# Decode attention over two KV caches: score products of the "D" heads shared between Pool and DVE, and the query weights laid into the V buffer

## The chip, the cores and the metric

The kernel runs on one core of a Trainium2 chip. Its time is the device time of one execution in microseconds (us). A profile is one execution; its span is 1.7 to 2.0 us shorter than the measured time of the same execution. The engines are named as the profile names them: PE does the matrix products, ACT and DVE copy, multiply and reduce, Pool multiplies, and SP issues the loads. SBUF is the memory that the loads fill; PSUM is the one that PE writes its products to.

## The reference, cut to what matters

Two independent problems, A and B, are the same single-token attention. Each has 32 heads, 8192 keys and a head size of 128, all bf16:

```python
q = (x @ wq).reshape(B, Sq, H, Dh).transpose(0, 2, 1, 3)          # x: 1 x 512, wq: 512 x 4096
scores = einsum("bhqd,bhkd->bhqk", q, k_cache) * Dh ** -0.5       # k_cache: 32 x 8192 x 128
o = einsum("bhqk,bhkd->bhqd", softmax(scores), v_cache)
out = o.transpose(0, 2, 1, 3).reshape(B, Sq, H * Dh) @ wo         # wo: 4096 x 512
```

There are 64 heads in all, and each needs a K block and a V block of 2 MB. Nothing is reused, so with the weights wq and wo 285 MB have to be read for a few vector products. The question of every such kernel is whether the loads ever stop.

## The kernel before

The heads go through in periods. In period g the K block of head g is loaded and its scores are computed, and the V block of head g - 12 is loaded and multiplied with its probabilities ("PV", on PE). Eight heads make a round, and each round has one softmax. K blocks go round in four buffers and V blocks in three. All loads are issued by SP in a fixed order, and a load first waits until the user of its buffer's former content is done:

```python
        def load_k(g):
            slot = g % NK                                  # NK = 4
            if g >= NK:
                ctr, val = k_free[g - NK]
                W('SP', ctr, val)
            ...
        def load_v(g):
            slot = g % NV                                  # NV = 3
            if g >= NV:
                W('SP', c_pv, pv_val[g - NV])
            ...
```

Scores are computed on one of two paths. A "P" head is transposed by PE, copied out of PSUM by ACT and multiplied by PE. A "D" head is multiplied with the broadcast query by Pool, in eight chunks of 128 x 1024, and reduced by DVE:

```python
            OP('POOL', lambda e, ...: e.tensor_tensor(
                ybuf[:, ys], kn[:, slot, i * CH:(i + 1) * CH, :],
                qbc[:, buf, qi:qi + 1, :].broadcast_to([P, CH, Dh]), ALU.mult
            ).then_inc(c_mul.sem, 1), "mul(%d,%d)" % (g, i))
            W('DVE', c_mul, mv)
            ...
            OP('DVE', lambda e, ...: e.tensor_reduce(
                s_sb[:, rb, j, i * CH:(i + 1) * CH], ybuf[:, ys], AX.X, ALU.add
            ).then_inc(c_red.sem, 1), "red(%d,%d)" % (g, i))
```

Which head takes which path is a string of 64 letters. Before, it is PPDPPDPPDPPD and then D and P by turns: 34 P heads and 30 D heads, head 62 D and head 63 P.

Each engine runs its own list of instructions in order. PE's list holds, one after the other, the transposes and score products of head g, the PV of head g - 12, and, now and then, the small products of a softmax. One of these, the transpose of the round's maxima, waits for DVE:

```python
        def plan_sm_tr(r, m1v):
            W('PE', c_m1, m1v)          # DVE's maxima of all eight heads of the round
            ...
            OP('PE', lambda e: e.transpose(misc[:, 0:P], m1pad[:], ident_f[:]).then_inc(c_x1.sem, 1), "smtr(%d)" % r)
```

Of the kernel before, what the change touches and what calls it, by code (L numbers as in the profile page):

```python
# [27 lines left out]
def _default_path(NG, G, LAG):  # L28
    pre = "PPDPPDPPDPPD"
    out = []  # L30
    for g in range(NG):
        if g < len(pre):
            out.append(pre[g])
        else:
            out.append("D" if (g % 2 == 0) else "P")
    return "".join(out)[:NG]


def bass_concat_heads__mha_block_cached__gqa_block_cached__decode_kernel(
# [15 lines left out]
    NV: int = 3,  # L55
# [4 lines left out]
    SMD: tuple = (2, 2, 2, 2, 2, 3, 2, 1),  # L60
):
# [5 lines left out]
    NA = 2  # L67
# [48 lines left out]
    with ExitStack() as st:  # L116
# [3 lines left out]
        vn = ec(nc.sbuf_tensor("vn", [P, NV, NT, Dh], BF16))  # L120
        ktsb = ec(nc.sbuf_tensor("ktsb", [P, NU, UT * P], BF16))
        ybuf = ec(nc.sbuf_tensor("ybuf", [P, NY, CH, Dh], BF16))
        wq_sb = ec(nc.sbuf_tensor("wq_sb", [P, NC_, H * Dh], BF16))
# [22 lines left out]
        y_acc = ec(nc.sbuf_tensor("y_acc", [1, NA, NOUT], F32))  # L146
        out_sb = ec(nc.sbuf_tensor("out_sb", [1, NA, NOUT], BF16))
        NKB = 3
        ktps = ec(nc.psum_tensor("ktps", [P, NKB, UT * P], BF16))
        sps = ec(nc.psum_tensor("sps", [P, 2, 512], F32))  # L150
# [19 lines left out]
        c_red = C("c_red")  # L170
        c_m1 = C("c_m1")
# [20 lines left out]

        def W(eng, ctr, val):
            if val is None or val <= 0:
                return
            prog[eng].append(lambda e, c=ctr, v=val: e.wait_ge(c.sem, v))
            DEBUG_PLAN.setdefault(eng, []).append("wait %s>=%d" % (ctr.name, val))
# [87 lines left out]
        def load_k(g):  # L285
            slot = g % NK
            if g >= NK:
                ctr, val = k_free[g - NK]
                W('SP', ctr, val)
# [4 lines left out]
        def load_v(g):  # L294
            slot = g % NV
            if g >= NV:
                W('SP', c_pv, pv_val[g - NV])
            a, h = divmod(g, H)
# [68 lines left out]
        def plan_T(g, u):  # L367
# [12 lines left out]
            if u == UPH - 1:  # L380
                k_free[g] = (c_t, tv)
# [47 lines left out]
        chunk_count = [0]  # L429

        def plan_D_chunk(g, i):
            n = chunk_count[0]
            chunk_count[0] = n + 1
            slot = g % NK
            ys = n % NY
# [3 lines left out]
            if i == 0:  # L439
                W('POOL', s_kn[slot], k_land[g])  # L440
                W('POOL', c_qbe, qbc_ready[g])
            if n >= NY:
                W('POOL', c_red, n - NY + 1)
            mv = c_mul.bump()
            assert mv == n + 1
            if i == NMC - 1:
                k_free[g] = (c_mul, mv)
            OP('POOL', lambda e, slot=slot, ys=ys, i=i, buf=buf, qi=qi: e.tensor_tensor(  # L448
                ybuf[:, ys], kn[:, slot, i * CH:(i + 1) * CH, :],
                qbc[:, buf, qi:qi + 1, :].broadcast_to([P, CH, Dh]), ALU.mult  # L450
            ).then_inc(c_mul.sem, 1), "mul(%d,%d)" % (g, i))
            W('DVE', c_mul, mv)
            if i == 0 and r >= 2:
                W('DVE', c_p, p_val[(r - 2) * G + G - 1])
            rv = c_red.bump()
            assert rv == n + 1
            if i == NMC - 1:
                red_last_val[g] = rv
            OP('DVE', lambda e, ys=ys, rb=rb, j=j, i=i: e.tensor_reduce(  # L459
                s_sb[:, rb, j, i * CH:(i + 1) * CH], ybuf[:, ys], AX.X, ALU.add  # L460
            ).then_inc(c_red.sem, 1), "red(%d,%d)" % (g, i))
# [189 lines left out]
        def plan_og_final(oi):  # L651
# [27 lines left out]
            if lastgrp:  # L679
                if first:  # L680
                    OP('DVE', lambda e: e.tensor_copy(out_sb[:, a, :], misc[0:1, 0:NOUT]).then_inc(c_y.sem, 1), "y(%d)" % oi)
                else:
                    OP('DVE', lambda e: e.tensor_tensor(out_sb[:, a, :], y_acc[:, a, :], misc[0:1, 0:NOUT], ALU.add).then_inc(c_y.sem, 1), "y(%d)" % oi)
                out_pending.append((a, yv))
            else:
                if first:
                    OP('DVE', lambda e: e.tensor_copy(y_acc[:, a, :], misc[0:1, 0:NOUT]).then_inc(c_y.sem, 1), "y(%d)" % oi)
# [222 lines left out]
```

## Time and profile before

| what | value | where it is read |
|---|---|---|
| time | 701.4 us (median of 3), 702.0 us (median of 15 in all) | runs |
| span of the profiled run | 703.0 us | page |
| bytes read, mean rate | 285.2 MB, 407 GB/s | page |
| DMA queue busy | 97.4% of the span | page |
| Pool, PE, ACT, DVE busy | 72, 72, 50, 45% | page |

These are the page's lines of busy time (us, share of the span, instructions), of the DMA queue (packets, MB, share of 16 engines), and of the two groups of the D path (busy us, mean ns of one, idle before it and what ended the idle time).

```profile
...
PE 505.2 (72%) x5915; PEld 325.7 (46%) x6000; DVE 314.1 (45%) x397; ACT 349.8 (50%) x583; POOL 504.1 (72%) x254
...
q1 hardware_dynamic: 28868, 285.23, 97.4%
...
L448 POOL TENSOR_TENSOR ybuf<-kn,qbc 128x1024 bf16<-128x1024 bf16 x240 | 499.8, 2119 | 129.6 <-DMA kn<-in_A_k_cache_dram 65.5
L459 DVE TENSOR_REDUCE s_sb<-ybuf 128x8 f32<-128x1024 bf16 x240 | 292.2, 1219 | 280.4 <-POOL ybuf L448 280.2
...
```

The DMA queue is nearly always busy and no engine is, so the loads bound the kernel. What can be won are the places where the loads stop. They are found by cutting the span into stretches of 5 us. This is the view of busy time by windows for the kernel before; the last three columns are the granted PE clock (as a share of the full clock), the DMA share and the GB/s.

```profile
...
core 0: us, PE busy (x) PEld busy (x) DVE busy (x) ACT busy (x) POOL busy (x), PEclk, DMA share, GB/s
...
55.00:60.00 5.00, 4.43 (x90) 3.46 (x88) 2.44 (x2) 5.00 (x7) 3.92 (x3) 1.00 0.61 202
...
600.00:605.00 5.00, 1.30 (x4) 0.48 (x5) 3.08 (x4) 0.00 (x0) 5.00 (x4) 0.55 1.00 423
...
635.00:640.00 5.00, 4.74 (x70) 3.04 (x68) 1.69 (x10) 3.50 (x4) 0.00 (x0) 1.00 0.60 206
...
665.00:670.00 5.00, 4.53 (x28) 1.99 (x28) 0.32 (x2) 0.90 (x2) 0.00 (x0) 1.00 0.88 311
...
```

The stretch from 600 us is what an undisturbed one looks like: a DMA share of 1.00 and 423 GB/s. From 55 to 60 us and from 635 to 640 us the loads were idle four tenths of the time, and from 665 to 670 us over one tenth. The next view lists what SP, which issues the loads, waited for (total us, times, longest).

```profile
...
SPq L238 <- PE acc L601: 468.8, 61, 12.9
SPq L238 <- PE ktps L387: 61.2, 14, 19.3
SPq L238 <- POOL ybuf L448: 41.6, 6, 14.6
...
```

SP waits nearly all the time, which is as it should be while loads are queued. It says who can make the loads stop: PE, which frees the V buffers (acc) and the K buffers of P heads (ktps), and Pool, which frees the K buffers of D heads. The same view cut to 34 to 62 us has one wait for Pool, of 10.6 us, and it belongs to the first D head: Pool needs 8 x 2.12 = 17 us for it, from 40.7 us on, and the next K load is issued at 57.4. The hole at 55 us is this wait.

To compare kernels at a given time I add up the bytes from stretches of 20 us (GB/s times 20 us). The kernel before has 38.9 MB at 100 us, 249.7 MB at 600 us and 273.4 MB at 660 us. One MB is 2.3 us at 427 GB/s.

### The profile page before, as it was taken

How to read it: one execution, taken by the hardware profiler on the slowest of the kernel's cores; microseconds unless marked ns; L12 is line 12 of the kernel's file. 1: busy time of each engine (PE TensorE's matmuls, PEld its weight loads, DVE VectorE, ACT ScalarE, POOL GpSimd, SP SyncE). 2: the span in 40 equal slices, each digit the busy share in tenths (PEclk: the TensorE clock that was granted, in tenths of full speed). 3: DMA queues.
4: the chain of work that ended last, by engine and by line, in shares of the span. 5: the costliest groups of instructions: out<-in, count | busy, mean ns of one | idle time of the engine just before them, and what ended most of it. 6: DMA issues, size and time to landing. Idle time of an engine off the chain costs nothing.

```text
span 703.0 us, 14000 instructions
## 1 busy us (share of the span) xinstructions
PE 505.2 (72%) x5915; PEld 325.7 (46%) x6000; DVE 314.1 (45%) x397; ACT 349.8 (50%) x583; POOL 504.1 (72%) x254
## 2 busy tenths in 40 slices
PE   1866567958687576767868675886777678769876
PEld 1765554725455343444535344553434445445332
DVE  0035446565454645444554534556454445542001
ACT  0837666727565272645625365552726457336010
POOL 2069799998788888876898858888787868980000
PEclk9967757968989898998989899898989989889999
DMA  8999999999999999999999999999999999998993
GB/s 338 420 413 356 412 407 425 398 428 413 430 427 410 427 430 423 429 413 426 425 424 415 420 425 426 427 412 428 425 429 414 400 428 424 428 412 345 382 418 149
DMA packets 28929, 286.11 MB, mean 407 GB/s; under 512 B 3266, under 2 KB 11460, under 8 KB 11460
## 3 DMA queue, kind: packets, MB, share of 16 engines
q1 hardware_dynamic: 28868, 285.23, 97.4%
q8 instruction: 47, 0.77, 0.4%
q14 instruction: 14, 0.11, 0.0%
HBM read 285.21 MB, written 0.00 MB: 406 GB/s over the span
## 4 chain that ended last, share of the span: by engine, by line
DMA 53%; POOL 18%; PE 15%; ACT 6%; issue 4%; DVE 1%; another core or an unknown queue 1%; SPq 1%; ACTq 0%; DVEq 0%
DMA kn<-in_B_k_cache_dram 25%; DMA kn<-in_A_k_cache_dram 22%; POOL ybuf L448 18%; PE acc L601 7%; DMA vn<-in_B_v_cache_dram 4%; PE ktps L387 4%; ACT ktsb L396 3%; PE misc L665 3%; ACT ptmp L546 2%; DMA wq_sb<-in_A_wq_dram 2%; PE sps L420 1%; SPq L238 1%; PE acc L312 1%; DVE s_sb L459 0%
## 5 line engine op out<-in xcount | busy, mean ns | idle before, releaser
L448 POOL TENSOR_TENSOR ybuf<-kn,qbc 128x1024 bf16<-128x1024 bf16 x240 | 499.8, 2119 | 129.6 <-DMA kn<-in_A_k_cache_dram 65.5
L459 DVE TENSOR_REDUCE s_sb<-ybuf 128x8 f32<-128x1024 bf16 x240 | 292.2, 1219 | 280.4 <-POOL ybuf L448 280.2
L396 ACT COPY ktsb<-ktps 128x1024 bf16<-128x1024 bf16 x272 | 264.3, 1023 | 70.3 <-PE ktps L387 63.5
L601 PE MATMUL acc<-vn,pt 128*128 128x512 bf16 x940 | 280.2, 414 | 20.3 <-DMA vn<-in_B_v_cache_dram 8.4
L387 PE MATMUL ktps<-ident,kn 128*128 128x128 bf16 x2176 | 181.7, 233 | 42.8 <-DMA kn<-in_B_k_cache_dram 25.6
L387 PEld LDWEIGHTS ktps<-ident,kn 128*128 128x128 bf16 x2176 | 153.2, 105 | 101.9 <-DMA kn<-in_B_k_cache_dram 33.1
L620 ACT CAST accsb<-acc 4x512 bf16<-4x512 f32 x64 | 36.6, 572 | 230.3 <-PE acc L601 224.5
L601 PEld LDWEIGHTS acc<-vn,pt 128*128 128x128 bf16 x1024 | 88.2, 105 | 86.8 <-issue 34.5
L420 PE MATMUL sps<-q_sb,ktsb 128*128 128x8 bf16 (+1 forms) x2176 | 95.9, 168 | 21.0 <-ACT ktsb L396 15.3
L420 PEld LDWEIGHTS sps<-q_sb,ktsb 128*128 128x128 bf16 x2176 | 83.9, 98 | 41.6 <-ACT ktsb L396 35.1
L665 PE MATMUL misc<-wo_sb,ot_pad 128*128 128x512 bf16 x64 | 26.8, 591 | 29.0 <-DVE ot_pad L648 29.0
L497 PE MATMUL misc<-ident_f,m1pad 128*128 128x128 f32 x8 | 3.6, 456 | 40.1 <-DVE m1pad L487 40.1
L648 DVE CAST ot_pad<-acc 128x1 bf16<-128x1 f32 x64 | 9.6, 150 | 50.4 <-PE acc L632 50.4
L665 PEld LDWEIGHTS misc<-wo_sb,ot_pad 128*128 128x128 bf16 x64 | 8.2, 136 | 45.0 <-DVE ot_pad L648 32.1
L577 ACT ACTIVATE pt<-ptmp,rinv 128x64 bf16<-128x64 f32 x64 | 16.1, 334 | 12.3 <-DVE rinv L564 12.3
L497 PEld LDWEIGHTS misc<-ident_f,m1pad 128*128 128x128 f32 x8 | 1.4, 176 | 44.1 <-DVE m1pad L487 44.1
L632 PE MATMUL acc<-ej,accsb 128*128 128x8 bf16 x256 | 16.2, 169 | 4.1 <-ACT accsb L620 1.8
L312 PE MATMUL acc<-xT,wq_sb 128*128 128x1 bf16 x256 | 7.0, 165 | 16.4 <-DMA wq_sb<-in_A_wq_dram 14.9
L324 DVE CAST q_sb<-acc 128x32 bf16<-128x32 f32 x2 | 0.4, 192 | 38.9 <-PE acc L312 38.9
L632 PEld LDWEIGHTS acc<-ej,accsb 128*128 128x128 bf16 x256 | 12.7, 100 | 10.2 <-ACT accsb L620 8.7
L344 ACT ACTIVATE diag<-ident,q 128x128 bf16<-128x128 bf16 x30 | 9.7, 403 | 12.6 <-DVE q L326 12.6
L312 PEld LDWEIGHTS acc<-xT,wq_sb 128*128 128x128 bf16 x256 | 6.9, 102 | 16.4 <-issue 16.4
(36 smaller groups left out, 86.3 us busy)
## 6 DMA issues: line engine op xcount, KB each, us to landing
kn<-in_A_k_cache_dram SPq DMA_DIRECT2D x32, 2048.0 KB, 18.0
vn<-in_A_v_cache_dram SPq DMA_DIRECT2D x32, 2048.0 KB, 15.6
kn<-in_B_k_cache_dram SPq DMA_DIRECT2D x32, 2048.0 KB, 19.3
vn<-in_B_v_cache_dram SPq DMA_DIRECT2D x32, 2048.0 KB, 13.6
wq_sb<-in_A_wq_dram SPq DMA_DIRECT2D x1, 4096.0 KB, 12.9
wq_sb<-in_B_wq_dram SPq DMA_DIRECT2D x1, 4096.0 KB, 17.2
wo_sb<-in_A_wo_dram SPq DMA_DIRECT2D x4, 1024.0 KB, 19.2
wo_sb<-in_B_wo_dram SPq DMA_DIRECT2D x4, 1024.0 KB, 18.8
```

The costliest lines, as they stand in the source:

```text
L312: last = e.matmul(acc[:, a, h:h + 1], wq_sb[:, c, h * Dh:(h + 1) * Dh], xT[:, a * NC_ + c:a * NC_ + c + 1], start=(c == 0), stop=(c == NC_ ...
L387: last = e.transpose(ktps[:, bank, i * P:(i + 1) * P], kn[:, slot, t, :], ident[:])
L396: OP('ACT', lambda e, bank=bank, ks_slot=ks_slot: e.copy(ktsb[:, ks_slot, :], ktps[:, bank, :]).then_inc(c_e.sem, 1), "evac(%d,%d)" % (g, u))
L420: last = e.matmul(sps[:, sb, col:col + nn], ktsb[:, ks_slot, i * P:(i + 1) * P], q_sb[:, g:g + 1].broadcast_to([P, nn]), start=True, stop= ...
L448: OP('POOL', lambda e, slot=slot, ys=ys, i=i, buf=buf, qi=qi: e.tensor_tensor(ybuf[:, ys], kn[:, slot, i * CH:(i + 1) * CH, :], qbc[:, buf ...
L459: OP('DVE', lambda e, ys=ys, rb=rb, j=j, i=i: e.tensor_reduce(s_sb[:, rb, j, i * CH:(i + 1) * CH], ybuf[:, ys], AX.X, ALU.add).then_inc(c_ ...
L546: OP('ACT', lambda e, r=r, j=j, g=g, rb=rb: e.activation(ptmp[:, rb, j, :], s_src(g), AF.Exp, bias=negb[:, r, j:j + 1], scale=scale, accum ...
L577: OP('ACT', lambda e, r=r, j=j, rb=rb: e.activation(pt[:, rb, j * NT:(j + 1) * NT], ptmp[:, rb, j, :], AF.Copy, scale=rinv[:, r, j:j + 1], ...
L601: last = e.matmul(acc[:, ob, :], pt[:, rb, j * NT + c * PVC:j * NT + c * PVC + P], vn[:, slot, c * PVC:(c + 1) * PVC, :].rearrange("p t d ...
L620: OP('ACT', lambda e, ob=ob: e.copy(accsb[0:PVC, ob, :], acc[0:PVC, ob, :]).then_inc(c_ac.sem, 1), "acccopy(%d)" % g)
L632: last = e.matmul(acc[:, ob, 0:NB], accsb[:, ob, jj * Dh:(jj + 1) * Dh], ej[:, jj:jj + 1].broadcast_to([P, NB]), start=(jj == 0), stop=(jj ...
L665: last = e.matmul(misc[:, 0:NOUT], ot_pad[:, g - r * G, :], wo_sb[:, r % 2, g - r * G, :], start=(i == 0), stop=(i == n - 1),)
```

## The change

Its intent: give Pool only six of a D head's eight chunks and let DVE multiply the other two, so that more heads (40 and not 30) can leave PE and ACT, and so that a D head frees its K buffer earlier. DVE reads the query from a copy in PSUM, which PE builds once per round. PSUM room for it comes from the transposes' buffer (two banks and not three). The query weights wq move into the space of the V buffers, which are idle while wq is needed; the room saved pays for a fourth V buffer.

```diff
-    pre = "PPDPPDPPDPPD"
+    pre = "PDPDPPDPDPDP"
...
-            out.append("D" if (g % 2 == 0) else "P")
+            out.append("P" if (g % 3 == 2) else "D")
...
-    NV: int = 3,
+    NV: int = 4,
...
+    DVC: int = 2,
...
+        wq_sb = vn[:, 0:WQS].rearrange("p s t d -> p (s t d)")[:, 0:NC_ * H * Dh].rearrange("p (c n) -> p c n", c=NC_)
...
-        wq_sb = ec(nc.sbuf_tensor("wq_sb", [P, NC_, H * Dh], BF16))
+        ybufe = ec(nc.sbuf_tensor("ybufe", [P, NYE, CH, Dh], BF16))
+        qrep = ec(nc.sbuf_tensor("qrep", [P, MAXD, P], BF16))
...
-        NKB = 3
+        NKB = 2
+        qps = ec(nc.psum_tensor("qps", [P, UT * P], BF16))
...
+            if g < WQS:
+                W('SP', c_q, q_done_val[NA - 1])
...
+                OP('DVE', lambda e, slot=slot, es=es, i=i, qs=qs: e.tensor_tensor(
+                    ybufe[:, es], kn[:, slot, i * CH:(i + 1) * CH, :],
+                    qps[:, None, qs * P:(qs + 1) * P].broadcast_to([P, CH, Dh]), ALU.mult
+                ).then_inc(c_dmul.sem, 1), "dmul(%d,%d)" % (g, i))
...
+            if r >= 1:                     # in the building of the PSUM copy for round r
+                prev = [h_ for rr in range(r) for h_ in round_D[rr]]
+                if prev:
+                    W('PE', c_dmul, dmul_val[(prev[-1], NMC - 1)])
```

The new path string makes head 62 a P head and head 63, the last one, a D head.

More of the change, by code (lines that the diff above doesn't have):

```diff
@@ L120, in bass_concat_heads__mha_block_cached__gqa_block_cached__decode_kernel @@
         vn = ec(nc.sbuf_tensor("vn", [P, NV, NT, Dh], BF16))
+        WQS = (NC_ * H * Dh + NT * Dh - 1) // (NT * Dh)
+        assert WQS <= NV
+        wq_sb = vn[:, 0:WQS].rearrange("p s t d -> p (s t d)")[:, 0:NC_ * H * Dh].rearrange("p (c n) -> p c n", c=NC_)
         ktsb = ec(nc.sbuf_tensor("ktsb", [P, NU, UT * P], BF16))
         ybuf = ec(nc.sbuf_tensor("ybuf", [P, NY, CH, Dh], BF16))
-        wq_sb = ec(nc.sbuf_tensor("wq_sb", [P, NC_, H * Dh], BF16))
+        NYE = 2
+        ybufe = ec(nc.sbuf_tensor("ybufe", [P, NYE, CH, Dh], BF16))
+        qrep = ec(nc.sbuf_tensor("qrep", [P, MAXD, P], BF16))
         wo_sb = ec(nc.sbuf_tensor("wo_sb", [P, 2, G, NOUT], BF16))
@@ L145, in bass_concat_heads__mha_block_cached__gqa_block_cached__decode_kernel @@
         rinv = ec(nc.sbuf_tensor("rinv", [P, NR, G], F32))
-        y_acc = ec(nc.sbuf_tensor("y_acc", [1, NA, NOUT], F32))
+        y_acc = ec(nc.sbuf_tensor("y_acc", [1, NOUT], F32))
         out_sb = ec(nc.sbuf_tensor("out_sb", [1, NA, NOUT], BF16))
-        NKB = 3
+        NKB = 2
         ktps = ec(nc.psum_tensor("ktps", [P, NKB, UT * P], BF16))
+        qps = ec(nc.psum_tensor("qps", [P, UT * P], BF16))
         sps = ec(nc.psum_tensor("sps", [P, 2, 512], F32))
@@ L170, in bass_concat_heads__mha_block_cached__gqa_block_cached__decode_kernel @@
         c_red = C("c_red")
+        c_dmul = C("c_dmul")
+        c_qr = C("c_qr")
+        c_qps = C("c_qps")
         c_m1 = C("c_m1")
@@ L191, in bass_concat_heads__mha_block_cached__gqa_block_cached__decode_kernel @@
         prog = {'SP': [], 'PE': [], 'ACT': [], 'DVE': [], 'POOL': []}
+        waited = {}
         def W(eng, ctr, val):
@@ L195, in W @@
                 return
+            key = (eng, ctr.name)
+            if waited.get(key, 0) >= val:
+                return
+            waited[key] = val
             prog[eng].append(lambda e, c=ctr, v=val: e.wait_ge(c.sem, v))
@@ L287, in load_k @@
             if g >= NK:
-                ctr, val = k_free[g - NK]
-                W('SP', ctr, val)
+                for ctr, val in k_free[g - NK]:
+                    W('SP', ctr, val)
             a, h = divmod(g, H)
@@ L380, in plan_T @@
             if u == UPH - 1:
-                k_free[g] = (c_t, tv)
+                k_free[g] = [(c_t, tv)]
             def op(e, g=g, u=u, bank=bank, slot=slot):
@@ L427, in plan_QK, with plan_D_step @@
             OP('PE', op, "QK(%d,%d)" % (g, u), UT)
-        chunk_count = [0]
-        def plan_D_chunk(g, i):
-            n = chunk_count[0]
-            chunk_count[0] = n + 1
+        NPC = NMC - DVC
+        DSTEP = max(0, NPC - DVC)
+        pool_chunks = [0]
+        e_chunks = [0]
+        red_of_pool = {}
+        red_of_e = {}
+        dmul_val = {}
+        e_idx = {}
+        qps_ready = {}
+        qps_slot = {}
+        def plan_D_step(g, u):
             slot = g % NK
-            ys = n % NY
             r, j = divmod(g, G)
@@ L438, in plan_D_chunk @@
             buf, qi = qbc_slot[g]
-            if i == 0:
-                W('POOL', s_kn[slot], k_land[g])
-                W('POOL', c_qbe, qbc_ready[g])
-            if n >= NY:
-                W('POOL', c_red, n - NY + 1)
-            mv = c_mul.bump()
-            assert mv == n + 1
-            if i == NMC - 1:
-                k_free[g] = (c_mul, mv)
-            OP('POOL', lambda e, slot=slot, ys=ys, i=i, buf=buf, qi=qi: e.tensor_tensor(
-                ybuf[:, ys], kn[:, slot, i * CH:(i + 1) * CH, :],
-                qbc[:, buf, qi:qi + 1, :].broadcast_to([P, CH, Dh]), ALU.mult
-            ).then_inc(c_mul.sem, 1), "mul(%d,%d)" % (g, i))
@@ L452, in plan_D_chunk @@
-            W('DVE', c_mul, mv)
-            if i == 0 and r >= 2:
-                W('DVE', c_p, p_val[(r - 2) * G + G - 1])
-            rv = c_red.bump()
-            assert rv == n + 1
-            if i == NMC - 1:
-                red_last_val[g] = rv
-            OP('DVE', lambda e, ys=ys, rb=rb, j=j, i=i: e.tensor_reduce(
-                s_sb[:, rb, j, i * CH:(i + 1) * CH], ybuf[:, ys], AX.X, ALU.add
-            ).then_inc(c_red.sem, 1), "red(%d,%d)" % (g, i))
+            if u == 0:
+                k_free[g] = []
@@ new lines, in plan_D_step @@
+            if DSTEP <= u < DSTEP + DVC:
+                i = NPC + (u - DSTEP)
+                ne = e_chunks[0]
+                e_chunks[0] = ne + 1
+                e_idx[(g, i)] = ne
+                es = ne % NYE
+                if i == NPC:
+                    W('DVE', s_kn[slot], k_land[g])
+                    W('DVE', c_qps, qps_ready[r])
+                if ne >= NYE:
+                    W('DVE', c_red, red_of_e[ne - NYE])
+                dv = c_dmul.bump()
+                dmul_val[(g, i)] = dv
+                if i == NMC - 1:
+                    k_free[g].append((c_dmul, dv))
+                qs = qps_slot[g]
+                OP('DVE', lambda e, slot=slot, es=es, i=i, qs=qs: e.tensor_tensor(
+                    ybufe[:, es], kn[:, slot, i * CH:(i + 1) * CH, :],
+                    qps[:, None, qs * P:(qs + 1) * P].broadcast_to([P, CH, Dh]), ALU.mult
+                ).then_inc(c_dmul.sem, 1), "dmul(%d,%d)" % (g, i))
@@ new lines, in plan_D_step @@
+            if u < NPC:
+                i = u
+                n = pool_chunks[0]
+                pool_chunks[0] = n + 1
+                ys = n % NY
+                if i == 0:
+                    W('POOL', s_kn[slot], k_land[g])
+                    W('POOL', c_qbe, qbc_ready[g])
+                if n >= NY:
+                    W('POOL', c_red, red_of_pool[n - NY])
+                mv = c_mul.bump()
+                assert mv == n + 1
+                if i == NPC - 1:
+                    k_free[g].append((c_mul, mv))
+                OP('POOL', lambda e, slot=slot, ys=ys, i=i, buf=buf, qi=qi: e.tensor_tensor(
+                    ybuf[:, ys], kn[:, slot, i * CH:(i + 1) * CH, :],
+                    qbc[:, buf, qi:qi + 1, :].broadcast_to([P, CH, Dh]), ALU.mult
+                ).then_inc(c_mul.sem, 1), "mul(%d,%d)" % (g, i))
+                W('DVE', c_mul, mv)
+                if i == 0 and r >= 2:
+                    W('DVE', c_p, p_val[(r - 2) * G + G - 1])
+                rv = c_red.bump()
+                red_of_pool[n] = rv
+                OP('DVE', lambda e, ys=ys, rb=rb, j=j, i=i: e.tensor_reduce(
+                    s_sb[:, rb, j, i * CH:(i + 1) * CH], ybuf[:, ys], AX.X, ALU.add
+                ).then_inc(c_red.sem, 1), "red(%d,%d)" % (g, i))
+                if DVC == 0 and i == NMC - 1:
+                    red_last_val[g] = rv
+            else:
+                i = u
+                ne = e_idx[(g, i)]
+                es = ne % NYE
+                W('DVE', c_dmul, dmul_val[(g, i)])
+                rv = c_red.bump()
+                red_of_e[ne] = rv
+                OP('DVE', lambda e, es=es, rb=rb, j=j, i=i: e.tensor_reduce(
+                    s_sb[:, rb, j, i * CH:(i + 1) * CH], ybufe[:, es], AX.X, ALU.add
+                ).then_inc(c_red.sem, 1), "red(%d,%d)" % (g, i))
+                if i == NMC - 1:
+                    red_last_val[g] = rv
@@ new lines, in plan_qps_build, with op, op2 @@
+        def plan_qps_build(r):
+            heads = round_D[r]
+            if not heads or DVC == 0:
+                return
+            a_need = max(h_ // H for h_ in heads)
+            bi = c_qr.n
+            W('ACT', c_qe, qe_val[a_need])
+            W('ACT', c_init, INIT_DONE)
+            if bi >= 1:
+                W('ACT', c_qps, bi)
+            qv = c_qr.bump()
+            for i, h_ in enumerate(heads):
+                last = (i == len(heads) - 1)
+                def op(e, i=i, h_=h_, last=last):
+                    ins = e.activation(qrep[:, i, :], ones_bf[:], AF.Copy, scale=q32[:, h_:h_ + 1])
+                    if last:
+                        ins.then_inc(c_qr.sem, 1)
+                OP('ACT', op, "qrep(%d)" % h_)
+                qps_slot[h_] = i
+            W('PE', c_qr, qv)
+            W('PE', c_init, INIT_DONE)
+            if r >= 1:
+                prev = [h_ for rr in range(r) for h_ in round_D[rr]]
+                if prev:
+                    W('PE', c_dmul, dmul_val[(prev[-1], NMC - 1)])
+            pv_ = c_qps.bump()
+            qps_ready[r] = pv_
+            def op2(e, n=len(heads)):
+                last = None
+                for i in range(n):
+                    last = e.transpose(qps[:, i * P:(i + 1) * P], qrep[:, i, :], ident[:])
+                last.then_inc(c_qps.sem, 1)
+            OP('PE', op2, "qps(%d)" % r, len(heads))
@@ L682, in plan_og_final @@
                 else:
-                    OP('DVE', lambda e: e.tensor_tensor(out_sb[:, a, :], y_acc[:, a, :], misc[0:1, 0:NOUT], ALU.add).then_inc(c_y.sem, 1), "y(%d)" % oi)
+                    OP('DVE', lambda e: e.tensor_tensor(out_sb[:, a, :], y_acc[:, :], misc[0:1, 0:NOUT], ALU.add).then_inc(c_y.sem, 1), "y(%d)" % oi)
                 out_pending.append((a, yv))
@@ L686, in plan_og_final @@
                 if first:
-                    OP('DVE', lambda e: e.tensor_copy(y_acc[:, a, :], misc[0:1, 0:NOUT]).then_inc(c_y.sem, 1), "y(%d)" % oi)
+                    OP('DVE', lambda e: e.tensor_copy(y_acc[:, :], misc[0:1, 0:NOUT]).then_inc(c_y.sem, 1), "y(%d)" % oi)
                 else:
-                    OP('DVE', lambda e: e.tensor_tensor(y_acc[:, a, :], y_acc[:, a, :], misc[0:1, 0:NOUT], ALU.add).then_inc(c_y.sem, 1), "y(%d)" % oi)
+                    OP('DVE', lambda e: e.tensor_tensor(y_acc[:, :], y_acc[:, :], misc[0:1, 0:NOUT], ALU.add).then_inc(c_y.sem, 1), "y(%d)" % oi)
         pend_qk = []
@@ L768, in build_qbc_for_round @@
                     if prev:
-                        ctr, val = k_free[prev[-1]]
-                        assert ctr is c_mul
-                        W('ACT', c_mul, val)
+                        for ctr, val in k_free[prev[-1]]:
+                            if ctr is c_mul:
+                                W('ACT', c_mul, val)
                 plan_qbc(grp, buf, idx)
@@ L807, in bass_concat_heads__mha_block_cached__gqa_block_cached__decode_kernel @@
                     qbc_built.add(r)
+            if g < NG and g % G == 0:
+                plan_qps_build(g // G)
             is_P = g < NG and path[g] == 'P'
@@ L814, in bass_concat_heads__mha_block_cached__gqa_block_cached__decode_kernel @@
                 if is_D:
-                    plan_D_chunk(g, u)
+                    plan_D_step(g, u)
                 if pend_qk and (len(pend_qk) > QLAG or not is_P):
```

## The prediction

> **What bounds the kernel now.** The DMA stream. The page shows queue 1 busy 97.4% of the span, 285.2 MB read at a mean of 407 GB/s; PE and Pool are busy 72%, ACT 50%, DVE 45%. Windows of 25 us in the undisturbed middle run at 424-431 GB/s with a DMA share of 1.00-1.02. That is near the 435 GB/s which the Trainium skill, "DMA: Bandwidth & Descriptors", Specifications, gives as the ceiling of a core's DMA engines; this trace agrees. At 427 GB/s the bytes alone need 668 us (estimate); the other 35 us:
> - start (about 3 us: 0-10 us has a DMA share of 0.71) and the work after the last V block (last bytes near 691.5, end 703): 12-13 us, untouched by the change;
> - early K phase, 40-100 us: mean 393 GB/s, about 4.8 us short of 427; the worst hole is 55-60 us (share 0.61): the next K load was held until 57.7 us by the first Pool head (from 40.7);
> - end, 620-690 us: mean 390, about 6 us short; worst holes at 635-640 (share 0.60) and 665-670 (0.88). V loads wait for PV of three heads earlier, and PE does that PV interleaved with the transposes of the last K head;
> - 100-620 us: about 7 us short, half of it wo loads, which stay.
>
> **What the change does, costed.** D heads go from 30 to 40, P heads from 34 to 24. Pool multiplies stay 240 (40 x 6 instead of 30 x 8), so Pool stays near 504 us, but one D head costs Pool 12.7 us instead of 17. DVE gets 80 more reduces (1.22 us: +97 us) and 80 multiplies; with one operand in PSUM I estimate 0.7-1.2 us each (+55 to +95): DVE 465-510 us. ACT loses 80 evacuations of 1.02 us (-82 us, plus about 16 for query copies); PE loses 640 transposes and 640 score matmuls (about -80 us busy).  With one SBUF input to it I expect Pool's multiply to stay at 2.12 us: the Trainium skill, "GPSIMD Engine Reference", Specifications, names two SBUF inputs or two-port modes as the contention (not shown here yet).
>
> **On the critical path.** Only the DMA holes. Early: D starts at head 1 (near 24 us instead of 41), heads release K buffers in 12.7 us or less: about 3 of 4.8 us return. End: head 63 becomes D, so PE's PV is no longer held behind its transposes, and V has four buffers: about 4 of 6 us return; the last softmax starts later after the last K (about 16 us instead of 11), which the fourth V buffer roughly covers. Middle: 0-1 us. In the middle, two D heads per three (29 us of DMA) ask about 25 us of Pool and 24 of DVE: tight, but inside the K ring. PE's wait for DVE at round starts (up to 9 us) is covered by four V buffers.
>
> **Prediction:** 694 us, 688 to 700 in 8 of 10. Faster by over 2% (under 687.4): 0.12; within 2%: 0.85; slower by over 2%: 0.03.
>
> **What would show it.** Right: DMA holes at 55-60 and 635-640 gone, middle windows unchanged at 424-431 GB/s, Pool multiplies 240 x 2.12 us, DVE near 490 us, ACT near 285, about 9-10 us between last bytes and end as before. Wrong steps: holes persist or move; middle windows drop below 420 GB/s with Pool or DVE busy throughout (score path now binding); DVE multiply over 1.3 us, or Pool multiply lengthened.
>
> **What would make it wrong.** Slower: Pool and DVE slowing one another, or DVE's in-order queue delaying PV or K release. Faster: the middle's short windows owing to shallow prefetch rather than to the loads themselves.

## The result, and the profile after

The changed kernel took 698.47 us (median of 12 runs, 697.64 to 699.47) beside 702.03 us (median of 15 runs) of the kernel before. The ratio is 0.994, with a 95% interval from 0.992 to 0.996: a small gain, clear of noise. The profiled run of the kernel before was one of its slower ones (704.75 us), so the spans, 703.0 and 696.5 us, overstate it. The same holds for every byte count of the kernel before below, since they come from this one profile.

The same lines of the page for the changed kernel, with the two new groups on DVE:

```profile
...
PE 467.2 (67%) x4698; PEld 287.1 (41%) x4767; DVE 445.9 (64%) x557; ACT 294.2 (42%) x560; POOL 504.2 (72%) x254
...
q1 hardware_dynamic: 28868, 285.23, 97.8%
...
L499 POOL TENSOR_TENSOR ybuf<-kn,qbc 128x1024 bf16<-128x1024 bf16 x240 | 499.9, 2120 | 128.6 <-DMA kn<-in_B_k_cache_dram 62.6
L508 DVE TENSOR_REDUCE s_sb<-ybuf 128x8 f32<-128x1024 bf16 x240 | 289.0, 1214 | 131.0 <-POOL ybuf L499 130.6
...
L520 DVE TENSOR_REDUCE s_sb<-ybufe 128x8 f32<-128x1024 bf16 x80 | 93.6, 1208 | 0.0
...
L481 DVE TENSOR_TENSOR ybufe<-kn,qps 128x1024 bf16<-128x1024 bf16 x80 | 54.1, 676 | 0.0
...
```

Pool does the same 240 multiplies at the same 2.12 us. DVE's share rises from 45 to 64%, ACT's falls from 50 to 42% and PE's from 72 to 67%. DVE's own multiply takes 0.68 us.

The windows of 5 us of the changed kernel:

```profile
...
55.00:60.00 5.00, 3.52 (x64) 3.34 (x62) 4.47 (x6) 4.92 (x7) 3.13 (x2) 0.83 1.01 429
...
630.00:635.00 5.00, 0.00 (x0) 0.00 (x0) 4.48 (x6) 0.00 (x0) 3.45 (x2) 0.50 1.00 426
635.00:640.00 5.00, 1.97 (x5) 0.82 (x6) 3.32 (x12) 0.30 (x1) 0.00 (x0) 0.50 0.88 374
640.00:645.00 5.00, 5.00 (x20) 2.20 (x19) 0.16 (x1) 1.30 (x7) 0.00 (x0) 0.62 0.41 118
645.00:650.00 5.00, 3.97 (x22) 1.68 (x22) 0.37 (x2) 3.21 (x18) 0.00 (x0) 1.00 0.86 357
...
```

The early hole is gone: from 55 to 60 us the loads run at 429 GB/s. Near the end a deeper one has opened, with 118 GB/s from 640 to 645 us. The first two lines show what came before it: PE did nothing from 630 to 635 us. The timeline tells why (its view runs from 612 to 662 us); each line is start, duration, engine, line, operation, and in brackets how long the engine had been idle and who ended that.

```profile
...
624.01 0.57 ACT L719 CAST accsb<-acc 4x512 bf16<-4x512 f32 x1 [3.71 <-PE acc L700]
...
626.62 0.95 PE L700 MATMUL acc<-vn,pt 128*128 128x512 bf16 x2 [2.64 <-DVE ot_pad L747]
...
634.62 2.33 DVE L520 TENSOR_REDUCE s_sb<-ybufe 128x8 f32<-128x1024 bf16 x2
...
638.03 0.48 PE L596 MATMUL misc<-ident_f,m1pad 128*128 128x128 f32 x1 [9.50 <-DVE m1pad L586]
...
638.30 5.33 PE L700 MATMUL acc<-vn,pt 128*128 128x512 bf16 x12
...
643.66 0.57 ACT L719 CAST accsb<-acc 4x512 bf16<-4x512 f32 x1 [4.50 <-PE acc L700]
...
```

In order: ACT's copy at 624.0 us ends the PV of head 51. PE starts the PV of head 52 at 626.6. At about 628.5 PE reaches the transpose of the last round's maxima in its list and stands before it for 9.5 us, until DVE has reduced the last chunks of head 63 (634.6) and taken the maxima. Only then does it go on with the PV of head 52, which is finished at 643.7 us, 15 us after PE began to wait. Three V buffers after it are loaded by then, SP waits for the fourth, and the loads run dry.

By bytes the changed kernel has 40.5 MB at 100 us (before: 38.9), 252.5 MB at 600 us (249.7) and 275.1 MB at 660 us (273.4). So it led by 1.6 MB at 100 us and by 2.8 MB at 600 us, and 1.1 MB of that lead was gone at 660 us. By 680 us it leads by 2.5 MB again (283.7 against 281.2), because the kernel before has its own hole at 665 to 670 us. The cost of the new hole is therefore better read against the same kernel without it, which a_lastP below provides.

### The profile page after: what moved, and what is told of

It is laid out like the page before. It is cut to its first block, busy times and chain, and to the rows that moved or that the text cites. A ratio compares the mean times of both kernels' runs of the same rounds, so it can differ in the third digit from the quotient of the medians. Undisturbed runs are those within 1.5% of the kernel's fastest.

```text
span 696.5 us, 11508 instructions
## 1 busy us (share of the span) xinstructions
PE 467.2 (67%) x4698; PEld 287.1 (41%) x4767; DVE 445.9 (64%) x557; ACT 294.2 (42%) x560; POOL 504.2 (72%) x254
## 3 DMA queue, kind: packets, MB, share of 16 engines
q1 hardware_dynamic: 28868, 285.23, 97.8%
## 4 chain that ended last, share of the span: by engine, by line
DMA 43%; POOL 20%; PE 20%; ACT 6%; DVE 6%; issue 3%; SPq 2%; POOLq 0%; another core or an unknown queue 0%; ACTq 0%
DMA kn<-in_B_k_cache_dram 25%; POOL ybuf L499 20%; DMA kn<-in_A_k_cache_dram 14%; PE acc L700 9%; PE ktps L405 5%; DVE s_sb L508 3%; ACT ktsb L414 2%; DVE s_sb L520 2%; PE misc L764 2%; DMA vn<-in_B_v_cache_dram 2%; DMA vn<-in_A_wq_dram 2%; SPq L254 2%; PE sps L438 1%; ACT diag L362 1%; ACT accsb L719 1%
## 5 line engine op out<-in xcount | busy, mean ns | idle before, releaser
L414 ACT COPY ktsb<-ktps 128x1024 bf16<-128x1024 bf16 x192 | 189.7, 1014 | 104.3 <-PE ktps L405 99.5
L405 PE MATMUL ktps<-ident,kn 128*128 128x128 bf16 x1536 | 141.9, 248 | 53.8 <-DMA kn<-in_B_k_cache_dram 29.2
L405 PEld LDWEIGHTS ktps<-ident,kn 128*128 128x128 bf16 x1536 | 118.5, 113 | 99.1 <-DMA kn<-in_B_k_cache_dram 32.6
L700 PEld LDWEIGHTS acc<-vn,pt 128*128 128x128 bf16 x1024 | 92.7, 105 | 92.8 <-issue 28.2
L520 DVE TENSOR_REDUCE s_sb<-ybufe 128x8 f32<-128x1024 bf16 x80 | 93.6, 1208 | 0.0
L438 PE MATMUL sps<-q_sb,ktsb 128*128 128x8 bf16 (+1 forms) x1536 | 68.7, 168 | 2.5 <-ACT ktsb L414 2.0
L438 PEld LDWEIGHTS sps<-q_sb,ktsb 128*128 128x128 bf16 x1536 | 63.3, 100 | 13.1 <-ACT ktsb L414 6.7
L481 DVE TENSOR_TENSOR ybufe<-kn,qps 128x1024 bf16<-128x1024 bf16 x80 | 54.1, 676 | 0.0
L558 PE MATMUL qps<-ident,qrep 128*128 128x128 bf16 x40 | 5.6, 306 | 47.1 <-DVE ybufe L481 37.7
L370 PE MATMUL misc<-diag,ones_bf 128*128 128x512 bf16 (+3 forms) x14 | 4.9, 353 | 23.4 <-ACT diag L362 23.4
```

The costliest lines, as they stand in the source:

```text
L405: last = e.transpose(ktps[:, bank, i * P:(i + 1) * P], kn[:, slot, t, :], ident[:])
L414: OP('ACT', lambda e, bank=bank, ks_slot=ks_slot: e.copy(ktsb[:, ks_slot, :], ktps[:, bank, :]).then_inc(c_e.sem, 1), "evac(%d,%d)" % (g, u))
L438: last = e.matmul(sps[:, sb, col:col + nn], ktsb[:, ks_slot, i * P:(i + 1) * P], q_sb[:, g:g + 1].broadcast_to([P, nn]), start=True, stop= ...
L481: OP('DVE', lambda e, slot=slot, es=es, i=i, qs=qs: e.tensor_tensor(ybufe[:, es], kn[:, slot, i * CH:(i + 1) * CH, :], qps[:, None, qs * P ...
L520: OP('DVE', lambda e, es=es, rb=rb, j=j, i=i: e.tensor_reduce(s_sb[:, rb, j, i * CH:(i + 1) * CH], ybufe[:, es], AX.X, ALU.add).then_inc(c ...
L700: last = e.matmul(acc[:, ob, :], pt[:, rb, j * NT + c * PVC:j * NT + c * PVC + P], vn[:, slot, c * PVC:(c + 1) * PVC, :].rearrange("p t d ...
```

## The experiments

Twelve kernels ran in three groups; each group had its own runs of the kernel before, with medians of 702.5, 703.5 and 702.4 us. The names begin with "a" for edits of the changed kernel and with "b" for edits of the kernel before. All gave correct results.

My theory after reading the traces was that the split and the new order closed the early holes and that the fourth V buffer mattered little (theory 1). The rival was that the V buffer did it all (2). For the end, the theory was PE's wait in front of PV (3).

### First group: which half made the gain, and what made the hole

**a_nv3**: the changed kernel with three V buffers.

```diff
-    NV: int = 4,
+    NV: int = 3,
```

> The changed kernel with three V buffers instead of four, everything else kept. Theory 1 (the gain came from the score path: shorter and earlier Pool heads close the holes of the first 140 us; the fourth V buffer matters little in the early part): the bytes moved by 100 us stay near 40.5 MB as in the changed kernel (38.9 MB before), and only the end loses, 1 to 4 us, total 699 to 703 us. Rival 2 (the deeper V buffer made the gain, the split only moved work): the time returns to that of the kernel before, about 702 us or more, and the middle, 100 to 620 us, falls from 424.0 back to about 421.7 GB/s.

Measured: 710.5 us, ratio to before 1.011 (1.008 to 1.014). Bytes at 100 us were 40.5 MB as theory 1 said, but at 600 us there were 247.4 and at 660 us 269.3 MB, less than in the kernel before. By the letter rival 2's "about 702 us or more" covers the time, but its reason doesn't: the middle, 100 to 620 us, fell to 414.3 GB/s and not back to 421.7. Neither theory had expected a kernel slower than the one before. Without the fourth V buffer the rest of the change costs 8 us. Windows of this run:

```profile
...
290.00:295.00 5.00, 4.85 (x78) 3.97 (x79) 0.76 (x1) 4.10 (x5) 5.00 (x3) 0.94 0.64 272
645.00:650.00 5.00, 2.21 (x6) 0.95 (x7) 3.08 (x12) 0.30 (x1) 0.00 (x0) 0.50 0.29 121
650.00:655.00 5.00, 4.90 (x22) 1.98 (x21) 0.16 (x1) 1.99 (x11) 0.00 (x0) 0.76 0.26 56
...
```

The early gain stays, the middle gets holes, and the one near the end, from 645 to 655 us, is almost a full stop. The waits of PE for DVE in this run (total us, times, longest) show three candidates: the wait before the PSUM query copy, the wait before the output product (for copies of PV results which stand in DVE's list behind reduces), and the wait before the round's maxima.

```profile
...
PE qps L558 <- DVE ybufe L481: 34.8, 4, 9.2
...
PE misc L764 <- DVE ot_pad L747: 31.4, 7, 8.7
PE misc L596 <- DVE m1pad L586: 23.6, 6, 10.3
...
```

**b_nv4**: the kernel before with wq in the V buffer and four V buffers, nothing else.

```diff
-    NV: int = 3,
+    NV: int = 4,
-        wq_sb = ec(nc.sbuf_tensor("wq_sb", [P, NC_, H * Dh], BF16))
+        wq_sb = vn[:, 0:WQS].rearrange(...)
+            if g < WQS:
+                W('SP', c_q, q_done_val[NA - 1])
```

> The kernel before with only wq laid into the V buffer and four V buffers; score path untouched. Theory 1: the hole at 55 to 60 us stays (38.9 MB by 100 us, as before), the end gains at most 2 to 3 us because V loads wait one head later: 699 to 702 us. Rival 2: all of the gain is here already, 698 to 699 us.

Measured: 698.2 us, ratio 0.993 (0.991 to 0.996). This is the whole size of the measured gain, without any split. Theory 1 was wrong in what it gave to the V buffer, but right about the place: the windows show that the early hole stays and that the late ones close, although the last head is still a P head here.

```profile
...
55.00:60.00 5.00, 4.46 (x88) 3.52 (x88) 2.44 (x2) 5.00 (x6) 3.90 (x3) 1.00 0.61 195
...
635.00:640.00 5.00, 4.74 (x43) 2.28 (x41) 1.56 (x10) 1.45 (x2) 0.00 (x0) 1.00 1.00 419
...
665.00:670.00 5.00, 4.78 (x26) 1.97 (x25) 0.16 (x1) 0.57 (x1) 0.00 (x0) 1.00 1.04 442
...
```

At 100 us there are 39.0 MB (before: 38.9), at 660 us 276.0 MB (273.4). The rival "the V buffer did it all" fits the total and still isn't the whole story, because the changed kernel has 1.5 MB more at 100 us. Two gains of about 4 us each exist, and the changed kernel shows only one in its total. So something took one back.

**a_lastP**: the changed kernel with the paths of heads 62 and 63 exchanged.

```diff
+    out[NG - 2:] = list("DP")
     return "".join(out)[:NG]
```

> The changed kernel with the paths of heads 62 and 63 exchanged, so that the last head goes over PE and not over Pool and DVE. Theory 3 (the end of the changed kernel lost what the start gained, because the maximum of the last round waits for the last D head, and PE's transpose of it stands in PE's order in front of the PV work that frees V buffers; PE stood still 9.5 us, and DMA fell to 118 GB/s at 640 to 645 us): the last softmax starts about 4 us earlier after the last K, the hole closes, 694 to 696 us. Rival 4 (the hole at 640 to 645 us is the price of four V buffers running dry whatever the order): no change, 698 us.

**a_late**: the changed kernel, with the last round's softmax planned eight steps later in the engines' lists.

```diff
-                        delayed.append([2, (lambda r=r: start_softmax(r))])
+                        delayed.append([10 if r == NR - 1 else 2, (lambda r=r: start_softmax(r))])
```

> The changed kernel with only the planned place of the last round's softmax moved eight steps later in the program orders of the engines; no work, buffer or path is changed. Theory 3: PE does the PV of head 52 before it waits for the last D head, the V loads are issued some 10 us earlier, the hole at 640 to 645 us closes, 694 to 696 us, although the last softmax itself starts no earlier. Rival 4: no change or slower, 698 to 700 us, since the softmax is what everything waits for.

Measured: a_lastP 693.4 us, ratio 0.987 (0.984 to 0.989); a_late 693.7 us, ratio 0.987 (0.984 to 0.990). Both close the hole, by different means, and both win 5 us against the changed kernel. The bytes say the same: a_lastP has the changed kernel's 252.5 MB at 600 us, but 285.8 MB and not 283.7 at 680 us, and 2.1 MB are 4.9 us. a_late is the sharper test: no head, buffer or amount of work differs. Its window in place of the hole, and PE's timeline there:

```profile
...
640.00:645.00 5.00, 4.69 (x23) 2.09 (x23) 0.16 (x1) 1.68 (x9) 0.00 (x0) 0.80 0.94 377
...
```

```profile
...
627.06 3.18 PE L700 MATMUL acc<-vn,pt 128*128 128x512 bf16 x14
637.09 1.01 PE L700 MATMUL acc<-vn,pt 128*128 128x512 bf16 x2 [6.84 <-DVE ot_pad L747]
...
638.85 0.42 PE L596 MATMUL misc<-ident_f,m1pad 128*128 128x128 f32 x1
...
```

PE does 14 products of the PV of head 52 at 627.1 us, ahead of its wait, where the changed kernel finished them at 643.7 us. The maxima come no earlier (638.85 against 638.03), and PE still stands idle for 6.8 us until 637: the PV of head 53 waits there for a copy on DVE (ot_pad), which stands in DVE's list behind the reductions of head 63. So the waits are not gone; what has changed is which PV is done before them. ACT's copy, which marks the end of a PV, came at 630.3 us for head 52 (643.7 in the changed kernel) and at 643.3 us for head 53 (648.8), so two V buffers came free some 13 and 5 us earlier. So theory 3 holds, and rival 4 falls: the loads ran dry because of an order in a list, not because the softmax came late.

### Second group: what the split, the order and the ten added D heads do

**a_nv3_qbc**: a_nv3, with DVE's multiplies reading the query from the SBUF copy that Pool uses.

```diff
-                    W('DVE', c_qps, qps_ready[r])
+                    W('DVE', c_qbe, qbc_ready[g])
-                    qps[:, None, qs * P:(qs + 1) * P].broadcast_to([P, CH, Dh]), ALU.mult
+                    qbc[:, buf, qi:qi + 1, :].broadcast_to([P, CH, Dh]), ALU.mult
...                        # and the PSUM copy is not built; the SBUF copy's reuse waits for DVE too
```

> The changed kernel with three V buffers, whose DVE multiplies read the query rows from the SBUF copy that Pool uses, so that the PSUM copy, and PE's wait for DVE before it (34.8 us in 4 waits), are gone. Theory 5 (that wait at the starts of the rounds is what made the changed kernel with three V buffers lose its middle, 414.3 against 421.7 GB/s of the kernel before): the middle rises to 420 to 424 GB/s and the time falls from 710.5 to 702 to 706 us, the hole at 645 to 655 staying. Rival 6 (other waits of PE for DVE, for the copies of PV results and for the round maxima, now behind a fuller DVE queue): little change, 708 to 711 us. Besides, Pool's multiply: if two SBUF inputs on DVE disturb Pool, 2.12 us becomes longer on average and DVE's 0.68 us multiply too; if not, both stay.

Measured: 715.8 us, ratio 1.017 (1.014 to 1.020), four to five us slower than a_nv3, a miss for both expectations. The groups of the page show a cost that I had asked about on the side:

```profile
...
L498 POOL TENSOR_TENSOR ybuf<-kn,qbc 128x1024 bf16<-128x1024 bf16 x240 | 526.2, 2229 | 114.0 <-DMA kn<-in_A_k_cache_dram 53.2
...
L480 DVE TENSOR_TENSOR ybufe<-kn,qbc 128x1024 bf16<-128x1024 bf16 x80 | 111.2, 1390 | 0.0
...
```

With both inputs in SBUF DVE's multiply takes 1.39 us on average and not 0.68 (single ones 0.68 to 2.41), and Pool's 2.23 us and not 2.12 (up to 2.59). The two engines disturb each other, and DVE pays most. (Both also read the same query tile in this run; no run separates that from the number of SBUF inputs.) That agrees with what the Trainium skill, "GPSIMD Engine Reference", Specifications, says of DVE instructions with two SBUF inputs, and it is the reason for the PSUM copy. As a test of theory 5 the run is inconclusive: PE's wait before the PSUM copy was gone, but with DVE slower, PE's wait for the maxima grew from 23.6 to 58.5 us:

```profile
...
PE misc L595 <- DVE m1pad L585: 58.5, 8, 12.3
...
```

A way to keep the copy in PSUM but to let the next round's rows go into other columns, so that PE needn't wait, was not run; what it would bring is not shown.

**a_pathb**: the changed kernel with the path string of the kernel before.

```diff
-    pre = "PDPDPPDPDPDP"
+    pre = "PPDPPDPPDPPD"
-            out.append("P" if (g % 3 == 2) else "D")
+            out.append("D" if (g % 2 == 0) else "P")
```

> The changed kernel (split multiplies, four V buffers) with the head paths of the kernel before: 30 D heads and not 40, last head on PE. Theory 7 (the ten added D heads bring nothing, because the middle is bound by the DMA stream; the split helps only in the early part, by shorter Pool heads, and the end wants a PE head last): Pool's busy time falls to about 385 us, the hole at the end is gone, and the time is 692 to 695 us. Rival 8 (moving heads from PE to D is what filled the early holes): the early hole at 55 to 60 us stays, 39 MB by 100 us, 697 to 699 us like the kernel before with four V buffers.

Measured: 695.0 us, ratio 0.987 (0.985 to 0.990); 40.5 MB at 100 us, no hole at the end, Pool busy 380 us (55%). The time is at the upper edge of theory 7, and rival 8 falls. The split alone brings the early gain at the old order, with Pool heads of 6 x 2.12 = 12.7 us. The ten added D heads are not needed for it. Whether they bring anything is not settled: a_lastP, with 40 D heads, has a median 1.6 us lower and 252.5 against 251.9 MB at 600 us, but the two ran in different groups, and their ratios to before are the same within their intervals (0.987 both).

**b_nv4_pre**: b_nv4 with the new order of the first twelve heads, but Pool doing all eight chunks.

```diff
-    pre = "PPDPPDPPDPPD"
+    pre = "PDPDPPDPDPDP"
```

> The kernel before with wq in the V buffer, four V buffers and the new order of the first twelve heads, but no split: Pool does all eight multiplies of a D head. Theory 7: five whole Pool heads of 17 us in the first 59 us of K loads cannot keep up, the early part gets no better than 39 MB by 100 us, probably worse (37 to 39), 698 to 703 us. Rival 9 (the early gain comes from the order alone, a D head at place 1 so that Pool starts at 25 and not at 41 us): 40 MB or more by 100 us, 694 to 696 us.

Measured: 698.4 us, ratio 0.992, as b_nv4; 38.6 MB at 100 us. The hole at 55 us is gone, but others open at 80 to 85 and 95 to 100 us (285 and 261 GB/s), when Pool has fallen behind. The order alone (with one D head more among the first twelve) brings nothing; rival 9 falls.

**a_dvc0**: the changed kernel with all eight chunks of its 40 D heads on Pool.

```diff
-    DVC: int = 2,
+    DVC: int = 0,
```

> The changed kernel with its paths (40 D heads) but all eight multiplies of a D head on Pool. Pool then needs 320 x 2.12 = 678 us, and it starts near 25 us and the end after the last head takes some 60 us: 750 to 775 us, bound by Pool. If it stayed near 698 us, Pool's rate would not matter at all, and the split would be needless.

Measured, in a single run: 769.3 us. The page says Pool:

```profile
...
PE 471.6 (61%) x4660; PEld 287.6 (37%) x4727; DVE 407.7 (53%) x477; ACT 281.7 (37%) x520; POOL 669.5 (87%) x334
...
L499 POOL TENSOR_TENSOR ybuf<-kn,qbc 128x1024 bf16<-128x1024 bf16 x320 | 665.2, 2127 | 37.2 <-DMA kn<-in_A_k_cache_dram 25.1
...
```

With 87% over a span that includes a start and an end without work for it, Pool is the bound. So 40 D heads need the split.

### Third group: the middle with three V buffers, the end in the other kernel, and a better version

**a_nv3_pathb**: both edits, three V buffers and the old path string, so that against the kernel before nearly only the split is new.

> The changed kernel with three V buffers and the head paths of the kernel before (30 D heads, last on PE), so that against the kernel before only the split itself is new. Theory 10 (what made 710.5 us of the changed kernel with three V buffers were its 40 D heads and their order, by waits of PE for DVE, not the split): 697 to 700 us, early part at 40.5 MB by 100 us, middle at 420 GB/s or more. Rival 11 (the split itself costs the middle, by DVE's fuller in-order queue and the PSUM copies): 703 us or more, the middle under 418 GB/s.

Measured: 700.2 us, ratio 0.996 (0.994 to 0.999), 0.2 us above the range of theory 10; 40.6 MB at 100 us, and a mean of 422.2 GB/s from 100 to 620 us (before: 421.7). The split doesn't cost the middle; rival 11 falls. The loss in a_nv3 came from the path string.

**a_nv3_roundP**: a_nv3, with the pattern DDPDDPDP in every round from head 12 on. Every round ends on a P head; there are 37 D heads and not 40.

```diff
-            out.append("P" if (g % 3 == 2) else "D")
+            out.append("DDPDDPDP"[g % 8])
```

> The changed kernel with three V buffers, and from head 12 on the pattern DDPDDPDP in each round of eight, so that every round ends on a PE head; 37 D heads and not 40. Theory 12 (PE loses the middle where a round ends on a D head, since PE then stands before the PSUM copy and the round maximum until DVE has done that head; the amount of D work is not the cause): 698 to 703 us, PE's wait for DVE before the PSUM copies falls from 34.8 to under 10 us, the hole at 645 to 655 us is gone, the middle at 420 GB/s or more. Rival 13 (the amount of D work delays PV wherever it stands): 705 to 710 us, the middle under 417 GB/s.

Measured: 700.8 us, ratio 0.999 (0.995 to 1.002): ten us better than a_nv3. PE's wait for DVE before the PSUM copies, 34.8 us, is gone altogether (the copies now wait only for ACT). The hole at 645 to 655 us is gone too (a shallower one, 326 to 357 GB/s from 635 to 645 us, is there). The middle is at 419.0 GB/s, short of the 420 that I had set but far from the 414.3 of a_nv3. PE's other waits for DVE remain or grow (from 31.4 and 23.6 us):

```profile
...
PE misc L764 <- DVE ot_pad L747: 51.4, 7, 9.4
PE misc L596 <- DVE m1pad L586: 29.0, 7, 5.3
...
```

The bytes put the gain in both places: 2.4 MB more than a_nv3 at 600 us, 5.5 MB more at 680 us, so the end has at least as large a part in it as the middle. So where the D heads stand in the round goes with most of the loss, and most of the rest of the middle's shortfall may be the output product's wait of 51.4 us, which no run removed. Since three D heads fewer also mean less Pool and DVE work, the share of the mere amount is not separated from this; a_nv3_pathb, with 30, has 422.2 GB/s.

**b_nv4_lastD**: b_nv4 with the paths of heads 62 and 63 exchanged, so that the last head is a D head.

```diff
+    out[NG - 2:] = list("PD")
     return "".join(out)[:NG]
```

> The kernel before with wq in the V buffer and four V buffers (698.2 us), with only the paths of heads 62 and 63 exchanged so that the last head is a D head of eight Pool multiplies. Theory 3 on the other kernel: PE stands before the last round's maximum until some 19 us after the last K, V loads stop, a hole of 3 to 8 us opens near 640 to 655 us: 701 to 706 us. Rival: no hole, 698 us, so the hole belonged to the split.

Measured: 705.2 us, ratio 1.004; seven us slower than b_nv4, by one exchange of two letters. The windows and PE's wait before the maxima near the end:

```profile
...
645.00:650.00 5.00, 4.07 (x10) 1.53 (x11) 1.22 (x9) 0.30 (x1) 0.00 (x0) 0.50 0.15 62
650.00:655.00 5.00, 4.20 (x22) 1.83 (x21) 0.16 (x1) 3.25 (x18) 0.00 (x0) 0.87 0.52 161
...
```

```profile
...
PE misc L502 <- DVE m1pad L492: 12.2, 1, 12.2
...
```

The hole follows the last D head into a kernel without any split, and is deeper there, which fits the last head's 17 us on Pool. Theory 3 holds on both kernels.

**a_best**: a_lastP, with the last V block loaded as two halves, each with its own semaphore, and the last round's output product cut so that one product and not seven stands within the last PV.

```diff
-            ogroups.append((r, heads[:-1]))
+            ogroups.append((r, heads[:-2]))
+            ogroups.append((r, heads[-2:-1]))
             ogroups.append((r, heads[-1:]))
...
+            if g == NG - 1:              # two loads of half a block, the second on s_vh
...
+            if g == NG - 1 and first == NPV // 2:
+                W('PE', s_vh, v_half[0])
```

> The changed kernel with the last head on PE (693.4 us), the last V block loaded as two halves with a semaphore each, and the output product of the last round cut into heads 56 to 61, 62 and 63 so that one product and not seven stands within the last PV. After the last bytes the other runs show 10 to 11 us. I expect about 2 us from the half block and 1 us from the shorter product: 690 to 692 us. If the end is instead bound by what follows the last PV, 693 us.

Measured: 692.6 us, ratio 0.986 (0.984 to 0.988), the fastest of all, but only 0.8 us better than a_lastP where I had expected up to 3. PE's timeline of a_lastP, and then of a_best, around the last PV:

```profile
...
682.70 0.60 PE L701 MATMUL acc<-vn,pt 128*128 128x512 bf16 x2 [1.14 <-DMA vn<-in_B_v_cache_dram]
...
684.11 1.67 PE L765 MATMUL misc<-wo_sb,ot_pad 128*128 128x512 bf16 x7
...
689.12 0.39 PE L765 MATMUL misc<-wo_sb,ot_pad 128*128 128x512 bf16 x1 [0.26 <-DVE ot_pad L748]
```

```profile
...
683.59 1.02 PE L712 MATMUL acc<-vn,pt 128*128 128x512 bf16 x4
684.45 0.38 PE L776 MATMUL misc<-wo_sb,ot_pad 128*128 128x512 bf16 x1
...
688.17 0.39 PE L776 MATMUL misc<-wo_sb,ot_pad 128*128 128x512 bf16 x1 [0.26 <-DVE ot_pad L759]
```

The output product within the last PV shrank from 1.67 to 0.38 us, as meant. The last PV itself starts no earlier: its first part stands behind the product of six heads that was moved in front of it, and behind the PV of head 62. About one us of three was won; no wait for either half of the block shows any more, since PE is still busy with what precedes.

## Why the prediction was right or wrong

The prediction, 694 us with a range from 688 to 700, held: 698.47 us lies inside, and the class "within 2%" is right. But the centre was 4.5 us too low. It forecast a gain of about 8 us, and about 4 came. That the number still lies inside the range is in part luck: the end gave nothing of its 4 us, and the middle, where 0 to 1 us was forecast, made up for part of that. The us below are estimates from the bytes of one profile each. They add up to 5.9 us, near the 6.4 us by which the two profiled runs differ and not the 3.6 us between the medians, so some 2 to 3 us of them are owed to the slow profiled run of the kernel before; the record doesn't show in which stage. Point by point:

- **The bound.** Right. The DMA queue was busy 97.4% of the span before and 97.8% after, and the windows show a hole in the loads closed where time was won early, and one opened where it was lost near the end.
- **Early, about 3 of 4.8 us return.** Right: 1.6 MB by 100 us, about 3.7 us. a_pathb shows that it is the split which brings this, b_nv4_pre that the order alone doesn't. So of the two reasons given, the shorter Pool heads carried it; the start at head 1 was not needed.
- **Middle, 0 to 1 us.** Too low. The lead grew from 1.6 to 2.8 MB between 100 and 600 us, that is by 1.2 MB or 2.8 us. b_nv4 has as good a middle (423.9 GB/s against 424.0, before 421.7), so the fourth V buffer is enough for it; its size is the least certain of these, since a_nv3_pathb, with three V buffers, already has 422.2 GB/s.
- **PE's waits at round starts are covered by four V buffers.** Right, as far as the middle shows it. Those waits exist (37.7 us in four in the middle of the changed kernel, the longest 10.7, as the line below shows), and the middle runs at 424.0 GB/s with them; a_nv3, with nearly the same waits (34.8 us) and three V buffers, has 414.3 and is 12 us slower.
- **End, about 4 of 6 us return; the late softmax "which the fourth V buffer roughly covers".** This is the step that failed. The mean from 620 to 680 us went from 382.7 to 378.7 GB/s, 0.2 MB or 0.6 us less. Nothing returned, although b_nv4 shows that the buffer alone would have given 418.0. The prediction had taken the last head's move off PE for a gain, but b_nv4 closes the late holes with head 63 still on PE, and the move opened a new one. I had counted how late the last softmax starts, and had not asked what stands behind it in PE's list: the PV work that frees the V buffers. a_lastP and a_late recover the term, 5 us, and land at 693.4 and 693.7 us, where the prediction had put the changed kernel.
- **Costs.** Pool's multiply at 2.12 us was right. DVE's multiply took 0.68 us, and DVE was busy 446 us and not the 490 expected. ACT at 294 us was near the 285. None of these bound anything.

The waits view of the changed kernel, PE only, from 110 to 620 us:

```profile
...
PE qps L558 <- DVE ybufe L481: 37.7, 4, 10.7
...
```

What the change is made of, then: the fourth V buffer is worth 4 to 5 us alone (b_nv4), the split about 2 us alone (a_nv3_pathb), both together 8 to 9 us with the old heads (a_pathb), which, given the intervals, is not clearly more than their sum; and the new path string, with its last head on Pool and DVE, took back 3.5 to 5 us of these (by the medians, 698.5 against 695.0 us, and by the ratios, 0.994 against 0.987).

## What to carry to other kernels

In a kernel bound by its loads, ask of every wait not only how long it is, but what stands behind it in the same engine's list and frees a buffer. A late result did little harm here once the release of a buffer went ahead of it, and moving one wait a few steps down the list was worth as much (5 us) as a whole 2 MB buffer was in the kernel before. Test the parts of a combined change singly and crossed: here one part was harmful without the other, and the total hid two gains and a loss of about the same size.

## What the Trainium skill lacked or had wrong

- "VectorE: DVE Perf Modes", the perf-mode tier table, puts a tensor_tensor with any PSUM operand at 1x. Here a bf16 product with one operand in SBUF and one in PSUM took 0.676 us for 1024 elements per partition. At the page's clock of 0.96 GHz, 1x would need 1.07 us (estimate), so the case ran faster than 1x. The text of the same page, "Why PSUM operands drop a tier", allows 2x for it and agrees; the table doesn't.
- "GPSIMD Engine Reference", Specifications, names the contention with a DVE instruction that has two SBUF inputs, but gives no size. Other pages of the skill treat which of the two engines waits; I found none with the size for this pair of products. Here DVE's product went from 0.68 to 1.39 us on average (0.68 to 2.41), Pool's from 2.12 to 2.23 (up to 2.59).
- "TensorE: Matmul & The Clock Gate", Part 1, says that an idle PE falls to half its clock and needs some us of work to return. The trace agrees and shows where it hurts: in the stretch with PE idle the granted clock was 0.50, and the first twelve products after it took 5.33 us, where fourteen took 3.18 at full clock in a_late. At that rate twelve would take 2.7 us (estimate), so this wait cost some 2.6 us more than its own 9.5. No page connects this with the release of buffers.
- I found no page which says that a wait in front of buffer-freeing work in an in-order list stops the loads; here it cost 5 us (698.5 against 693.4 us) in the changed kernel and 7 us (705.2 against 698.2) in the other.
